# Decays in their own stage, the last product of block zero later, and scan products in two pieces

## The chip, the cores and the metric

The kernel runs on one core of one Trainium2 chip. The metric is the device time of one execution in microseconds; each kernel is run several times and the median counts. The engines are named as in the profile: PE is TensorE's matmul side and PEld its weight loads, DVE is VectorE, ACT is ScalarE, POOL is GpSimd, SP is SyncE, which here only issues DMAs. Each engine works through its own queue in order; semaphores tie the queues together.

## What is computed

A Mamba-2 scan (4 batches, 8 heads, 768 tokens, head size 32, state size 16) and then, on its output seen as 3072 tokens of 256 values, a two-layer network with an ELU between the layers:

```python
for c in range(nc):                      # chunks of tokens, per batch and head
    cum = np.cumsum(la, axis=-1)         # la = log(a)
    L = np.exp(cum[:, :, :, None] - cum[:, :, None, :]) * causal
    M = np.einsum('bhin,bhjn->bhij', Cc, Bc) * L
    y_intra = np.einsum('bhij,bhjd->bhid', M, xc)
    y_inter = np.einsum('bhin,bhnd->bhid', Cc, state) * np.exp(cum)[:, :, :, None]
    y[:, :, sl] = y_intra + y_inter
    state = decay_full * state + sum_j(Bc * xc * decay_from_j)
...
h = x @ w_in                             # 3072 x 256 by 256 x 2048
g = np.where(h > 0, h, np.exp(np.minimum(h, 0)) - 1)
out = g @ w_out                          # 3072 x 2048 by 2048 x 256
```

The weights come as 64-bit floats; the kernel reads them as two 32-bit words and makes 32-bit floats of them itself.

## The kernel before

**Blocks.** The 3072 tokens are 12 blocks of 256 (n = 0 to 11), each with all 8 heads of one batch. Blocks 0 to 3 go singly, then in pairs (4, 5), (6, 7), (8, 9), (10, 11). The order of all work is written out by hand: the kernel sets its own schedule, and each engine runs its instructions in the order in which the program issues them.

**The scan of a block.** `spread_cum` (L377) has SP load the tile L, the running sums of the logarithms spread over 128 partitions, from a scratch tensor `flat`. `decay_of(n, h)` (L518) turns one head of L into decays: two ACT activations at L521, and after every fourth head two causal masks on POOL at L526; `decay(n, q)` does two heads. L has two buffers. `scores` (L532) forms the products of C and B on PE (L541) and `weigh` (L546) multiplies them by L on DVE (L550) into M. `sums` and `states` carry the state along (PE L571, DVE L588, POOL L593). `across` (L604) multiplies the carried state on PE (L616) into four PSUM tiles ps_y, and `inside` (L624) adds the products of M and x to the same tiles (L635), first for t = 0 and then for t = 1 (four heads each), and copies each half out into yT with ACT (L652). `turn_part` transposes and masks B and C on DVE (L453, L461, L444), and `scaled` (L402) scales B on POOL (L408).

**The weights.** They come in 16 pieces. `w_take(i, low)` takes the two words apart: |high word| on ACT (L196), the low word on the engine that it is given (L205 on ACT or L209 on DVE), the sign on DVE (L223). `w_give` puts them together: DVE L231 and L238, then POOL L248. `words_of_w` (L731) and `low_of_w` (L741) split a finished piece of w_in into two words for the first layer of the pairs: ACT L736, DVE L737 and POOL L843.

**The first layer.** For single blocks `l1` (L659, PE L667) followed by `elu` (ACT L680, L687, DVE L689). For pairs `l1_words(n, m)` (L777): six matmuls at L787 into two PSUM tiles (ps_w and ps_h), ACT L791, then DVE L808 of the step before (`end_words`), DVE L794, and with `begin_end` ACT L800 and L801. It reads words of y that `words_of_y` (L750: ACT L755, DVE L759, L762) and `both_of_y` (DVE L772) make.

**The second layer.** `l2(n, j)` (PE L827) for blocks 0 and 1, with an ACT copy (L833) and a store at the end of a block. For pairs `second` (L866) is a generator of small steps of four matmuls each (L902), with sums of its operands on POOL (L843) and of its results on DVE (L880).

**The order around the change.** The loop over j = 0 to 7 (L1171) runs the second layer of block 0 (`l2(0, j)`) beside the first layer of blocks 2 and 3, takes the last pieces of w_out (at j = 0, 2, 3, 4 and 5), and calls `scan_ahead` (L1139), which prepares the scan of blocks 4 and 5. The loop over j = 8 to 15 (L1216, with i = j - 8) runs the first layer of the pair (2, 3). Then comes one stage for each pair, n = 4, 6, 8, 10 (L1298), of 16 steps k: `l1_words(n, k)`, `turn_step`, `stage_scan(n, k)` for the pair m = n + 2 (L1277), `begin_end`, and some steps of `second(n - 2)` by `l2s`. In step 9 the pair m is scored and weighed, in step 13 come `across` and `inside`. In step 10 `stage_scan` loads the tile L of the pair after m, and in steps 11 and 12 it computes that pair's first two `decay`s.

PSUM has seven buffers with the tag "a", shared by the tiles of the first layer, every second product sum of the second layer, and the scan's tiles; an eighth holds the other product sums.

Of the kernel before, what the change touches and what calls it, by code (L numbers as in the profile page):

```python
# [32 lines left out]
def kernel(  # L33
# [27 lines left out]
    nc = tc.nc  # L61
# [3 lines left out]
    NP = NB * NG  # L65
# [35 lines left out]
    st = {}  # L101
# [411 lines left out]
    def decay(n, q):  # L513

        decay_of(n, 2 * q)
        decay_of(n, 2 * q + 1)
# [104 lines left out]
                            tile_position=(32 * q, col), skip_group_check=True)  # L621
        return y

    def inside(y, *ns):  # L624


        for t in range(2):
            for at, n in enumerate(ns):
                s = st[n]
                for u in range(2):  # L630
                    for v in range(2):
                        toks = slice(Q * v, Q * v + Q)
                        for q in range(4):
                            h, col = 4 * t + q, (D * q + shift(n, v)) % P
                            nc.tensor.matmul(  # L635
                                out=y[t][v][col:col + D, at, u],
                                lhsT=s["x"][toks, u, D * h:D * (h + 1)],
                                rhs=s["M"][h // 2][toks, u, h % 2], start=False, stop=True,
                                tile_position=(Q * v, col), skip_group_check=True)
            n = ns[0]  # L640
            if n // 2 not in yT:
                yT[n // 2] = ffn.tile([P, KC, 2, 2, P], F32, tag="yT", name="yT")
            out = yT[n // 2][:, t, n % 2:n % 2 + len(ns)]
            for v in range(2):
                k = shift(n, v)
                for at in (0, k) if k else (0,):
                    count, src = P - k, (at + k) % P
                    to, src = out[at:at + count, :, :, Q * v:Q * v + Q], y[t][v][src:src + count]
                    if t and n == 1:
                        nc.vector.tensor_copy(to, src)  # L650
                    else:
                        nc.scalar.copy(out=to, in_=src)  # L652
        for n in ns:
            st.pop(n)


    g_of = {}
# [73 lines left out]
    def words_of_w(i):  # L731

        w = pieces[i][0]
        k_words[i] = conv.tile(
            [P, 2, KC, CW], F32R, tag="w64", name="w_words", bufs=W_AHEAD)
        nc.scalar.activation(k_words[i][:, 0], w, ACT.Copy, scale=NEAR)  # L736
        nc.vector.scalar_tensor_tensor(  # L737
            out=k_words[i][:, 1], in0=k_words[i][:, 0].bitcast(F32), scalar=1.0 / WORD - 1.0,
            in1=w, op0=ALU.mult, op1=ALU.add)
# [224 lines left out]
    def w_take(i, low):  # L964

        w_abs(i)
        w_low(i, low)
        w_sign(i)
# [38 lines left out]
    y = across(0)  # L1007
# [81 lines left out]
    todo = 5  # L1089
# [49 lines left out]
    def scan_ahead(i):  # L1139

        m = 4
        if i < 2:
            load_b(m + i)
            load_bc(m + i)
            spread_exp(m + i)
        if i == 2:
            spread_cum(5)
            load_x(m)
            load_x(m + 1)
        if 1 < i < 8:  # L1150
            decay(m + i // 6, (i - 2) % 4)
        for part in {3: (0,), 4: (1,), 6: (2, 0), 7: (1,)}.get(i, ()):
            turn_part(m + (i // 6 if part < 2 else 0), part)

# [15 lines left out]

    for j in range(2 * DIRECT):  # L1171
        n, i = 2 + j // DIRECT, j % DIRECT
        l2(0, j)
        piece = todo < len(pieces) and j != 1
        if j == 0:
            elu()
        if piece:
            w_take(todo, nc.scalar if j > 1 else nc.vector)
        l1(n, i)
        if j == 0:  # L1180
            scaled(3, nc.gpsimd)
            turn(3)
            elu()
            turn_exp(3)
        if piece:
            w_give(todo)
            todo += 1
        while lag:
            elu()
        if j == 0:  # L1190
            decay(3, 2)
            decay(3, 3)
        if j == 1:
            scores(3)
            sums(3)
            for q in range(4):
                weigh(3, q)
        if j == 2:
            states(3)
        if j == 3:  # L1200
            inside(across(3), 3)
        if j == 4:
            words_of_y(2)
        if j == 5:
            both_of_y(2)
        scan_ahead(j)
        if j == 3:
            s_out[:] = weight_sums()
        if j == 5:
            words_of_w(4)  # L1210
        if j == 6:
            low_of_w(4)
            differences(0, 4)
        if j == 7:
            words_of_w(5)
    for j in range(8, 16):  # L1216
        i = j - 8
        l1_words(2, j)
        if i == 7:
            words_of_y(4)  # L1220
        for p in ((), (6,), (), (7,), (0,), (1,), (2,), ())[i]:
            words_of_w(p)
        for p in ((5,), (), (6,), (7,), (0,), (), (), ())[i]:
            low_of_w(p)
        if i < 2:
            decay(5, i + 2)
        if i == 7:
            l2(1, 6)
            l2(1, 7)
        begin_end()  # L1230
        if i == 0:
            turn_part(5, 2)
            scaled(4, nc.gpsimd)
            scaled(5, nc.gpsimd)
        if i < 2:
            load_bc(i + 6)
            l2(1, i)
        if i == 2:
            turn_part(4, 3)
            turn_part(5, 3)  # L1240
            scores(4, 5)
            sums(4, 5)
            for q in range(4):
                weigh_two(4, q)
            l2(1, 2)
            states(4)
            states(5)
            for to in (6, 7):
                load_b(to)
                spread_cum(to)  # L1250
        if i == 3:
            l2(1, 3)
        if i == 4:
            l2(1, 4)
            y = across(4, 5)
            inside(y, 4, 5)
        if i == 5:
            l2(1, 5)
        if i in (0, 1, 3, 4):
            sum_t1(2, (0, 1, 3, 4).index(i), nc.vector)  # L1260
        if i in (4, 6):
            turn_part(6, i // 2 - 2)
        if i in (2, 5):
            differences(4 if i == 2 else 6, 2)
        if i < 6:
            sum_weights(nc.gpsimd, a_out, s_out, i)
# [10 lines left out]
    def stage_scan(n, k):  # L1277

        m = n + 2
        if k < 2:  # L1280
            spread_exp(m + k)
        if k == 2:
            load_x(m)
            load_x(m + 1)
        for h in range((5 + 3 * k) // 2, (8 + 3 * k) // 2) if 0 < k < 9 else ():
            decay_of(m + h // NH, h % NH)
        if k in (11, 12) and m + 2 < NP:
            decay(m + 2, k - 11)
        if k in (7, 8):
            scaled(m + k - 7, nc.gpsimd)  # L1290
        if k in (6, 7) and m + 2 < NP:
            load_bc(m + k - 4)
        if k == 10 and m + 2 < NP:
            for to in (m + 2, m + 3):
                load_b(to)
                spread_cum(to)

    for n in range(4, NP, 2):  # L1298
        m = n + 2 if n + 2 < NP else None
        steps = second(n - 2)  # L1300

        def l2s(count):
            for _ in range(count):
                next(steps)

        for k in range(16):
            l1_words(n, k)
            if m and k == 15:
                words_of_y(m)
            turn_step(n, k // 2 * 2 + 1, k % 2)  # L1310
            if n == 4 and k == 0:
                decay(6, 1)
            if n == 4 and 1 < k < 5:
                for _ in range(2):
                    next(left)()
            if m:
                stage_scan(n, k)
            begin_end()
            if k == 0 and n > 4:
                store(n - 4, 0)  # L1320
                store(n - 4, 1)
            if not m:
                l2s(4 if k % 2 else 3)
                continue
            l2s((3 + (n == 4), 3 - (n == 4), 3, 3, 3, 3, 3, 3, 4, 5, 2, 2, 3, 1, 3, 0)[k])
            if k == 9:
                scores(m, m + 1)
                sums(m, m + 1)
                for q in range(4):
                    weigh_two(m, q)  # L1330
                l2s(2)
                states(m)
            if k == 10:
                states(m + 1)
            if k == 13:
                y = across(m, m + 1)
                l2s(2)
                inside(y, m, m + 1)
        if m:
            l2s(4)  # L1340
            both_of_y(m)
        end_words()
        for _ in steps:
            pass
    n = NP - 2
# [34 lines left out]
```

## Time and profile before

| | us |
|---|---|
| median of 3 runs (352.72 to 353.66) | 353.25 |
| the profiled execution | 352.38 |
| its span | 350.4 |
| PE busy | 341.2 |
| DVE busy | 258.3 |
| ACT busy | 237.7 |
| POOL busy | 216.8 |

The span runs from the first to the last instruction in the trace; the profiled execution's own time has 2.0 us around it. PE's granted clock is full in the whole span. A row of the timeline has the start and the time in us, the engine, the line and operation, what it writes and reads, the number of like instructions in a row, and in brackets how long the engine was idle before it and what released it. PE's times are pipelined: one matmul lasts longer than the step to the next.

### The profile page before, as it was taken

What the parts mean: (1) busy time and instruction counts of PE and PEld (TensorE: products, weight loads), DVE (VectorE), ACT (ScalarE), POOL (GpSimd) and SP (SyncE); (2) the same over time, 40 slices, a digit from 0 to 9 for tenths busy, and PEclk for the clock granted to TensorE, in tenths of its full rate; (3) what the DMA queues carried; (4) which work ended last, traced back from release to release, by engine and by line L of the source; (5) the groups of instructions that cost most, each with busy time, mean ns of one, the idle gap of its engine ahead of it and who ended that gap; (6) DMA issues with size and microseconds to landing.
All of it is one profiled execution on the core that took longest, in us unless ns stands there. A gap on an engine that the chain in (4) does not pass through costs nothing.

```text
span 350.4 us, 9866 instructions
## 1 busy us (share of the span) xinstructions
PE 341.2 (97%) x3878; PEld 299.1 (85%) x3878; DVE 258.3 (74%) x511; ACT 237.7 (68%) x541; POOL 216.8 (62%) x338
## 2 busy tenths in 40 slices
PE   8899999999999999999999999999999999999996
PEld 5578888887778899888889988998988999999996
DVE  3998979879997898855878775888684757565232
ACT  4789989797668889567599467589547566665000
POOL 5554554539999699965196766095854074355860
PEclk9999999999999999999999999999999999999999
DMA  8978988461250510170431070230000100001001
GB/s 152 266 183 220 266 188 216 117 107 54 54 137 2 123 44 18 13 155 4 105 61 32 9 159 4 83 54 2 2 0 4 63 0 3 0 0 38 25 1 61
DMA packets 72726, 26.48 MB, mean 76 GB/s; under 512 B 57768, under 2 KB 67560, under 8 KB 72680
## 3 DMA queue, kind: packets, MB, share of 16 engines
q1 hardware_dynamic: 70360, 25.60, 31.3%
q8 instruction: 30, 0.49, 0.6%
q10 hardware_dynamic: 2320, 0.26, 0.5%
q14 instruction: 16, 0.13, 0.1%
HBM read 22.51 MB, written 3.34 MB: 74 GB/s over the span
## 4 chain that ended last, share of the span: by engine, by line
PE 62%; ACT 10%; DVE 7%; SPq 6%; DMA 5%; POOL 5%; issue 4%; POOLq 0%; ACTq 0%; DVEq 0%
PE ps_o L902 27%; PE ps_h L787 12%; PE ps_h L667 7%; PE ps_w L787 7%; PE ps_o L827 3%; DMA L<-flat 3%; SPq L116 2%; ACT L L521 2%; SPq L178 2%; PE ps_y L635 2%; ACT e L800 2%; DVE ps_h L794 2%; ACT e L801 1%; POOL g L843 1%; DMA bc<-in_C_dram 1%
## 5 line engine op out<-in xcount | busy, mean ns | idle before, releaser
L902 PEld LDWEIGHTS ps_o<-w_out,g 128*128 128x128 f32 x640 | 78.6, 192 | 3.4
L902 PE MATMUL ps_o<-w_out,g 128*128 128x128 f32 x640 | 80.1, 276 | 0.0
L808 DVE SCALAR_TENSOR_TENSOR g<-e,ps_h 128x512 f32<-128x512 f32 x72 | 49.3, 685 | 33.4 <-ACT e L801 32.9
L800 ACT ACTIVATE e<-ps_h 128x512 f32<-128x512 f32 x72 | 43.0, 597 | 44.6 <-DVE ps_h L794 44.6
L843 POOL TENSOR_TENSOR g<-g 128x256 f32<-128x256 f32 x36 | 26.3, 731 | 55.1 <-DVE g L808 55.1
L794 DVE SCALAR_TENSOR_TENSOR ps_h<-ps_h,e 128x512 f32<-128x512 f32 x72 | 50.1, 695 | 12.5 <-ACT e L791 9.5
L791 ACT ACTIVATE e<-ps_w 128x512 f32<-128x512 f32 x72 | 42.2, 586 | 20.0 <-PE ps_w L787 19.9
L787 PE MATMUL ps_w<-y_both,w_words 128*128 128x512 f32 x144 | 52.2, 440 | 0.5 <-DVE M L550 0.2
L801 ACT ACTIVATE e<-e 128x512 f32<-128x512 f32 x72 | 45.5, 631 | 2.3
L667 PE MATMUL ps_h<-yT,w_in 128*128 128x256 f32 (+1 forms) x208 | 45.3, 368 | 1.6 <-POOL w_in L248 1.6
L787 PE MATMUL ps_h<-y,w_words 128*128 128x512 f32 x144 | 45.6, 398 | 0.0
L787 PE MATMUL ps_h<-y,w 128*128 128x512 f32 x144 | 44.6, 391 | 0.0
L521 ACT ACTIVATE L<-L,ncum 128x64 f32<-128x64 f32 x160 | 42.8, 337 | 2.2 <-DMA L<-flat 1.5
L667 PEld LDWEIGHTS ps_h<-yT,w_in 128*128 128x128 f32 x208 | 36.5, 191 | 7.1 <-POOL w_in L248 2.3
L902 PE MATMUL ps_o<-w_sum,g 128*128 128x128 f32 x304 | 38.5, 276 | 0.1
L902 PEld LDWEIGHTS ps_o<-w_sum,g 128*128 128x128 f32 x304 | 37.1, 192 | 1.6 <-ACT e L791 0.5
L526 POOL TENSOR_SCALAR_AFFINE_SELECT L<-L 64x512 f32<-64x512 f32 x40 | 28.5, 712 | 14.3 <-ACT L L521 13.0
L787 PEld LDWEIGHTS ps_h<-y,w 128*128 128x128 f32 x144 | 27.1, 188 | 6.3
L787 PEld LDWEIGHTS ps_h<-y,w_words 128*128 128x128 f32 x144 | 26.8, 188 | 6.1 <-issue 0.4
L843 POOL TENSOR_TENSOR g<-t,g 128x256 f32<-128x256 f32 x40 | 28.1, 736 | 5.8 <-PE ps_o L902 5.7
L827 PE MATMUL ps_o<-w_out,g 128*128 128x256 f32 x128 | 30.5, 383 | 0.5 <-POOL w_out L248 0.5
L843 POOL TENSOR_TENSOR g<-g,t 128x256 f32<-128x256 f32 x40 | 29.6, 773 | 0.0
(134 smaller groups left out, 540.7 us busy)
## 6 DMA issues: line engine op xcount, KB each, us to landing
L<-flat SPq DMA_DIRECT2D x20, 256.0 KB
w<-in_moe_w_out_dram SPq DMA_DIRECT2D x8, 512.0 KB
w<-in_moe_w_in_dram SPq DMA_DIRECT2D x7, 512.0 KB
xr<-in_x_dram SPq DMA_DIRECT2D x24, 128.0 KB
out_dram<-c_sum SPq DMA_DIRECT2D x9, 256.0 KB
bc<-in_B_dram SPq DMA_DIRECT2D x24, 64.0 KB
bc<-in_C_dram SPq DMA_DIRECT2D x22, 64.0 KB
ec<-flat_exp SPq DMA_DIRECT2D x10, 128.0 KB
```

Of the source, the lines that this page charges most:

```text
L521: nc.scalar.activation(L[:, h, u], L[:, h, u], ACT.Exp, bias=ncum[:, u, row:row + 1])
L526: nc.gpsimd.affine_select(out=part, in_=part, pattern=[[0, 4], [0, 2], [1, Q]], compare_op=ALU.is_ge, fill=0.0, base=0, channel_multiplier=-1)
L667: nc.tensor.matmul(out=ps[:, j, toks], lhsT=w_in[i][:, k, j * P:(j + 1) * P], rhs=yT[n // 2][:, k, n % 2].rearrange("p u i -> p (u i)")[:, ...
L787: nc.tensor.matmul(out=ps, lhsT=lhs[:, k], rhs=rhs[:, k], start=k == 0 and lhs is not w0, stop=k == KC - 1 and lhs is not w1)
L791: nc.scalar.activation(e, both, ACT.Copy, scale=WORD)
L794: nc.vector.scalar_tensor_tensor(out=high, in0=high, scalar=WORD - 1.0, in1=e, op0=ALU.mult, op1=ALU.add)
L800: nc.scalar.activation(e, high, ACT.Relu, scale=-1.0)
L801: nc.scalar.activation(e, e, ACT.Exp, scale=-1.0)
L808: nc.vector.scalar_tensor_tensor(out=g_of[n, m].rearrange("p b i -> p (b i)"), in0=e, scalar=1.0, in1=h, op0=ALU.subtract, op1=ALU.max)
L827: nc.tensor.matmul(out=o_of[n][:, ts], lhsT=g_of[n, j][:, m % 2, ts * P:(ts + 1) * P], rhs=w_out[:, m], start=(m == 0 and ts == 0), stop=( ...
L843: nc.gpsimd.tensor_tensor(out=out, in0=in0, in1=in1, op=ALU.subtract)
L902: nc.tensor.matmul(out=ps[:, ts], lhsT=b[:, ts * P:(ts + 1) * P], rhs=a[:, i], start=(i == chunk[0] and ts == 0), stop=(i == chunk[-1]), s ...
```

## The change

- `inside` can be called for one t alone. In step 13 of the stages n = 4, 6 and 8 the two steps of the second layer that stood between `across` and `inside` are parted: one ahead of each half of `inside`.
- In the stages n = 6 and 8 all 16 heads of the pair m are decayed in steps 1 to 8, two in each. Before, four of them came in steps 11 and 12 of the stage before, and the other 12 in steps 1 to 8. Stage n = 4 keeps its 12 heads, and has no decays in steps 11 and 12.
- The eight decays of blocks 4 and 5 all come in the loop over j = 2 to 7 (1, 2, 1, 2, 1, 1 of them); before, six came there, one each, and two in the next two steps (i = 0, 1).
- In that loop the low words of the pieces at j = 2 to 5 are made by DVE, not by ACT; `words_of_w(4)` comes at j = 4 and `low_of_w(4)` at j = 5 (before: at the end of j = 5, and at j = 6); and `l2(0, 7)` comes behind `l1(3, 3)`.

The number of instructions on PE is the same. On DVE there are four more and on ACT four fewer.

```diff
-    def inside(y, *ns):
-        for t in range(2):
+    def inside(y, *ns, t=None):
+        for t in range(2) if t is None else (t,):
...
-        for n in ns:
-            st.pop(n)
+        if t:
+            for n in ns:
+                st.pop(n)
...
     def scan_ahead(i):
-        if 1 < i < 8:
-            decay(m + i // 6, (i - 2) % 4)
+        for q in {2: (0,), 3: (1, 2), 4: (3,), 5: (4, 5), 6: (6,), 7: (7,)}.get(i, ()):
+            decay(m + q // 4, q % 4)
...
     for j in range(2 * DIRECT):
         n, i = 2 + j // DIRECT, j % DIRECT
-        l2(0, j)
+        if j < 7:
+            l2(0, j)
         piece = todo < len(pieces) and j != 1
         if j == 0:
             elu()
         if piece:
-            w_take(todo, nc.scalar if j > 1 else nc.vector)
+            w_take(todo, nc.vector)
         l1(n, i)
+        if j == 7:
+            l2(0, j)
...
         if j == 4:
             words_of_y(2)
+        if j == 4:
+            words_of_w(4)
+        if j == 5:
+            low_of_w(4)
         if j == 5:
             both_of_y(2)
         scan_ahead(j)
...
-        if j == 5:
-            words_of_w(4)
         if j == 6:
-            low_of_w(4)
             differences(0, 4)
...
-        if i < 2:
-            decay(5, i + 2)
...
     def stage_scan(n, k):
-        for h in range((5 + 3 * k) // 2, (8 + 3 * k) // 2) if 0 < k < 9 else ():
+        heads = ((5 + 3 * k) // 2, (8 + 3 * k) // 2) if n == 4 else (2 * k - 2, 2 * k)
+        for h in range(*heads) if 0 < k < 9 else ():
             decay_of(m + h // NH, h % NH)
-        if k in (11, 12) and m + 2 < NP:
-            decay(m + 2, k - 11)
...
             if k == 13:
                 y = across(m, m + 1)
-                l2s(2)
-                inside(y, m, m + 1)
+                l2s(1)
+                inside(y, m, m + 1, t=0)
+                l2s(1)
+                inside(y, m, m + 1, t=1)
```

## The prediction

> **What bounds the kernel now.** I read the page's busy times first, then the timeline of PE alone from 45 us on, then the waits of the stretches in which PE pauses, then the timelines of ACT, DVE and POOL there.
>
> ```profile
> PE 341.2 (97%) x3878; PEld 299.1 (85%) x3878; DVE 258.3 (74%) x511; ACT 237.7 (68%) x541; POOL 216.8 (62%) x338
> ```
>
> PE is the bound: only its pauses can be won. Taking each MATMUL's start less the usual step between its kinds (111 ns between two L902 products, 146 ns from L635 to L787), the pauses after 45 us are 0.7 at 79.6, 0.5 at 92.5, 0.8 at 95.5, 0.7 at 104.4, 0.5 at 115, 1.7 from 156 to 160.6, 0.4 at 170, 0.95 from 210 to 214, 0.15 at 222 and 0.8 at 267: 7.2 us, the most that any reordering can bring. Three rows of PE's timeline, with the idle time and its releaser behind them, are the ones to know:
>
> ```profile
> 79.64 2.00 PE L827 MATMUL ps_o<-w_out,g 128*128 128x256 f32 x8 [0.53 <-POOL w_out L248]
> 157.26 0.68 PE L616 MATMUL ps_y<-bct,Sx 32*64 32x64 f32 x36 [0.51 <-DVE p_sum L880]
> 267.13 0.46 PE L635 MATMUL ps_y<-M,xr 64*32 64x64 f32 x33 [0.62 <-issue]
> ```
>
> **Part 1: no decays of the next pair in steps 11 and 12 of stage n = 4.** ACT and DVE there, from their timelines:
>
> ```profile
> 153.34 1.07 ACT L521 ACTIVATE L<-L,ncum 128x64 f32<-128x64 f32 x4 [1.52 <-DMA L<-flat]
> 155.46 0.58 ACT L791 ACTIVATE e<-ps_w 128x512 f32<-128x512 f32 x1
> ```
> ```profile
> 152.10 0.69 DVE L794 SCALAR_TENSOR_TENSOR ps_h<-ps_h,e 128x512 f32<-128x512 f32 x1
> 155.59 0.69 DVE L808 SCALAR_TENSOR_TENSOR g<-e,ps_h 128x512 f32<-128x512 f32 x1 [2.79 <-ACT e L801]
> 156.79 0.42 DVE L880 TENSOR_TENSOR p_sum<-ps_o,p_sum 128x256 f32<-128x256 f32 x1
> ```
>
> ACT reaches step 11's decays, waits 1.52 us for a transfer of L that was issued only at 148.1, and everything behind it in its queue (L800, L801, the next L791) is late; so DVE's L808, L794 and L880 are late; and L880 frees the PSUM buffer that PE's products at L616 want, hence the pause at 157.26. Without the decays: DVE's L794 ends at 152.79, L800 starts at 152.85 instead of 154.31, the next L791 at 154.0 instead of 155.46, L794 at 154.7, L880 at 155.3 to 155.7, before the 155.99 at which PE begins L616. PE then runs L616 without a pause, as it does in stage n = 8, which has no such decays: there the stretch from the step before L616 (262.86) to step 14 (267.52) takes 4.66 us, in n = 4 5.55 (155.46 to 161.01); n = 4 has 16 products of 13 ns fewer (0.2). Step 14 starts at about 160.05: 0.95 won. ACT's copies out of ps_y start at 159.25 instead of 160.70, so y_both is 1.45 earlier, PE only 0.95, and the 0.37 at 170 goes to about 0.05. Together 1.3 us, with 0.8 (L880 still a little late) and 1.6 as ends. What is late next is the fetch pause of part 4, counted in the 4.66.
>
> **Part 2: the same removal in stage n = 6.** Here it brings nothing: the decays lie in a wait that is there anyway.
>
> ```profile
> 206.67 1.06 ACT L521 ACTIVATE L<-L,ncum 128x64 f32<-128x64 f32 x4 [0.49 <-POOL Sx L593]
> 207.67 0.60 ACT L800 ACTIVATE e<-ps_h 128x512 f32<-128x512 f32 x1
> ```
> ```profile
> 206.94 0.69 DVE L794 SCALAR_TENSOR_TENSOR ps_h<-ps_h,e 128x512 f32<-128x512 f32 x1
> 210.17 0.42 DVE L880 TENSOR_TENSOR p_sum<-ps_o,p_sum 128x256 f32<-128x256 f32 x1
> ```
>
> L794 ends at 207.63, so L800 can't start before 207.67 with or without decays; DVE is late on its own, after eight L550 and eight L588. I take 0, with 0.4 as the end (that pause gone).
>
> **Part 3: 16 heads instead of 12 in steps 1 to 8 of n = 6 and n = 8.** Four L521 take 0.95 us and lie where ACT waits for L794. A step with four runs 2.60 us from L791 to L791 (176.32 to 178.92), one with two 2.63 (173.44 to 176.32, less 0.25 for the L914 copy in it); PE's step is 2.72. So 0; if that cover failed, 0.25 a step in four more steps, less the 0.1 of slack in each, would cost 0.6 a stage. POOL gets two L526 (1.4 us) more between 178 and 200, where it idles about 4 us (1.96 and 2.06 are its two longest); its next queue entry, four L843, ends at 182.6 instead of 181.1, and PE wants it at 187.98. 0.
>
> **Part 4: the scan products in two pieces.** PE's pauses within L635 (0.28, 0.47 and 0.83 in the three stages) have no releaser but "issue".
>
> ```profile
> q8 instruction: 30, 0.49, 0.6%
> ```
>
> These are 30 packets of 16 KB; one starts in the trace at 211.72 and PE resumes 2.37 us later, one at 264.47 and it resumes 2.66 later: PE has run through its instructions before the next block is there. The split puts four of eight L902 products later, but all eight are still between the start of that packet and the pause, so PE resumes at the same time. The one change of kind added (205 ns into L635, 146 out, less the steps saved: 0.23 us) goes into the pause; so does the 0.16 pause at 212.1. I take 0. Ends: 0.7 lost (3 x 0.23, not covered), 1.3 won (both later pauses gone). The Trainium skill, Runtime: NRT & Kernel Launch, Instruction fetch mechanics, says that blocks of 256 instructions are fetched while the one before runs and that this is mostly hidden. By that rule there is no pause to hide the 0.23 in, and the sum would be 0.7 lower; the rows above speak against it.
>
> **Part 5: loop of block zero, 57 to 97 us.** The change moves four low words (L205, 0.75 each) from ACT to DVE (L209: 0.42 median, 0.87 longest), puts L737 of w_words(4) ahead of the last w_out piece on DVE, puts eight L521 (2.0) instead of four into ACT at j = 3 and 5, and block zero's last product behind l1(3,3), 1.73 us later.
>
> ```profile
> 71.76 0.43 DVE L231 TENSOR_SCALAR mag<-mag 128x512 f32<-128x512 f32 x1 [1.61 <-ACT mag L196]
> 77.48 0.69 DVE L238 SCALAR_TENSOR_TENSOR mag<-mag,sgn 128x512 uint32<-128x512 uint32 x1
> 78.31 1.28 POOL L248 TENSOR_TENSOR w_out<-mag,w_out 128x512 uint32<-128x512 uint32 x1 [3.62 <-DVE mag L238]
> ```
>
> Of the four L209 two hide in DVE's 1.61 idle. The L196 of j = 4 comes after eight L521 at about 72.05 instead of 71.06; from the L231 behind it (72.65) DVE runs without idle: the old 6.4 us to the end of L238, less 0.3 idle, plus L737 0.93 and one L209 0.45: 80.1. POOL's L248 ends at 81.4. The product, now due at 80.7, waits 0.7 again: the move of 1.73 is eaten, and l1_words(2, 8) starts at about 83.1 (83.01 before). Behind it ACT's ob copy and L680 are 0.45 late; SP's store waits on that copy, and behind it stand the loads of bc(6), first read at 104.6, so they are covered. Taking the two decays out of the next two steps gives ACT 0.45 back (L800 at 90.66 waits for L521, L794 was done at 90.17), so the products after the weighing (95.50) move by about 0.2 later. Without any DVE contention 0.6 earlier, with L209 at 0.87 and L737 at 1.23 2.0 later. I take 0.2 lost, near the median rows. The Trainium skill, SBUF: State Buffer, two separate sides, says that DVE in a two-port mode and POOL lock each other out for a whole instruction, which speaks against moving L209 to DVE. It agrees with two L772 that took 2.51 us beside POOL's L526 and 1.28 alone.
>
> **Sum.** 1.3 + 0 + 0 + 0 - 0.2 = 1.1 us. The profiled execution took 352.38 (span 350.4), 0.87 under the median of 353.25: 351.3 against itself, 352.1 as a median.
>
> **Rivals.** *More*: the split does end the fetch pauses, or the last product is no longer waited for (0.47 + 0.83, or 0.7, or both): 350.1 to 351.4. For it: the split spreads the small products; against: the pause depends on the packet, and the same products lie before it. *DVE becomes the bound at j = 4 and 5*: each us that L238 of the last piece ends after 80.1 goes to PE whole; from 1.3 us late on it eats the gain of part 1; at the upper price (2.0 for 0.2) the time is 353.9, and 355 if two L772 at 1.25 each and L737, next in DVE's queue and read by l1_words(2, 8), are late by another 1.1. For it: DVE has no idle from 74 to 84; against: POOL, the other side of contended rows, is idle from 74.7 to 78.3. *Nothing*: the 1.7 at 156 is kept by DVE as in n = 6: 353.3.
>
> **Numbers.** Mine (351.5 to 352.8) 0.57, more 0.21, DVE 0.15, nothing 0.07. A measurement can tell 0.3%, 1.06 us. Faster: 0.31 of mine and all of "more": 0.52. Slower than 354.3: DVE's upper end, 0.09. The same: 0.39. Range 350.7 to 353.7, which leaves out the low end of "more" and the top of "DVE".
>
> **What would show it.** Right: no DMA wait at L521, L616 in n = 4 unbroken, step 14 less than 5 us after step 13's last product; pauses in L635 still there in all three stages; L827's wait for L248 still there, near 80.7. Wrong: L635 unbroken; PE pauses at L787 in steps 1 to 9 of n = 6; l1_words(2, 8) a microsecond from 83.

## The result, and the profile after

The changed kernel takes **351.92 us** (median of 18 runs, 351.15 to 353.13), the kernel before 353.04 on the same chips (18 runs, 351.95 to 353.86): a ratio of **0.9974, 95% interval 0.9962 to 0.9985**, or 1.1 us less. The profiled execution took 351.6 us, its span is 349.5. PE is still the bound (first row: busy time, share, instructions), and the DMA wait at L521 is gone: the second row, of the costliest groups, ends with the idle time ahead of the group, 0.2 us in all, where it had been 2.2 with 1.5 of it for the load of L.

```profile
PE 340.5 (97%) x3878; PEld 298.1 (85%) x3878; DVE 259.7 (74%) x515; ACT 234.7 (67%) x537; POOL 217.2 (62%) x338
...
L521 ACT ACTIVATE L<-L,ncum 128x64 f32<-128x64 f32 x160 | 42.2, 336 | 0.2
```

The changed kernel's L634 is L635 of before and its L651 is L652; L616, L667, L787 and L902 keep their numbers. PE's timeline of the changed kernel has the rows that answer to those of before:

```profile
81.87 1.99 PE L827 MATMUL ps_o<-w_out,g 128*128 128x256 f32 x8 [1.01 <-POOL w_out L248]
...
91.50 0.50 PE L787 MATMUL ps_h<-y,w 128*128 128x512 f32 x1 [0.20 <-POOL w L843]
...
156.56 0.83 PE L616 MATMUL ps_y<-bct,Sx 32*64 32x64 f32 x48
...
160.22 0.46 PE L634 MATMUL ps_y<-M,xr 64*32 64x64 f32 x31 [0.34 <-issue]
...
213.16 0.65 PE L634 MATMUL ps_y<-M,xr 64*32 64x64 f32 x40 [0.49 <-issue]
...
265.80 0.46 PE L634 MATMUL ps_y<-M,xr 64*32 64x64 f32 x33 [0.24 <-issue]
```

L616 of n = 4 runs unbroken, all three pauses in the scan products are still there, block zero's last product waits longer than before (1.01, was 0.53), and one wait is new, at 91.50.

The single traces differ by up to 0.9 us before the first edit acts (PE's ninth product L827 starts between 54.98 and 55.84 in all traces of this study), and the last stage, which has no edit, varies by 0.5. So I compare stretches. *Loop*: from that ninth product to the `ps_w` product at 118.1, less the fetch pause at 104, which is there in every kernel. *n = 4*, *n = 6*, *n = 8*: between two `ps_w` products, the same ones in every kernel (154.31 to 177.44, 205.75 to 230.80 and 258.98 to 283.83 in the trace of before).

| us | loop | n = 4 | n = 6 | n = 8 | ratio of times to before (95%) |
|---|---|---|---|---|---|
| before | 61.99 | 23.12 | 25.05 | 24.85 | 1 |
| changed kernel | 62.65 | 21.63 | 24.79 | 24.72 | 0.9974 (0.9962 to 0.9985) |
| stage_decays | 61.97 | 21.80 | 24.85 | 24.71 | 0.9959 (0.9948 to 0.9971) |
| split_only | 62.03 | 22.54 | 25.25 | 24.88 | 1.0003 (0.9988 to 1.0017) |
| loop_only | 62.60 | 22.39 | 25.29 | 24.63 | 1.0012 (0.9996 to 1.0028) |
| no_loop | 61.99 | 21.64 | 24.85 | 24.95 | 0.9958 (0.9946 to 0.9970) |
| late_product | 62.00 | 21.72 | 24.84 | 25.01 | 0.9961 (0.9945 to 0.9976) |
| late_plus_decays | 61.76 | 21.63 | 25.12 | 24.71 | 0.9948 (0.9930 to 0.9967) |
| late_plus_low | 62.24 | 21.62 | 25.06 | 24.71 | 0.9962 (0.9946 to 0.9979) |
| late_plus_words | 62.22 | 21.75 | 24.91 | 24.72 | 0.9974 (0.9962 to 0.9986) |
| wide_split | 61.98 | 21.81 | 24.86 | 25.07 | 0.9980 (0.9965 to 0.9995) |
| wide_best | 61.72 | 21.81 | 24.85 | 25.07 | 0.9956 (0.9938 to 0.9974) |
| pre_split | 61.97 | 22.03 | 25.06 | 25.43 | 0.9992 (0.9980 to 1.0003) |
| two_chains | 61.98 | 21.91 | 24.37 | 24.84 | 0.9943 (0.9921 to 0.9965) |

The loop column repeats within 0.06 among kernels with the same loop, so 0.2 can be read there. Between the two traces of before and after the span fell by 0.93: n = 4 gave 1.49, n = 6 0.26, n = 8 0.13, and the loop took 0.66 back; the rest (the start 0.25 earlier, the pause at 104 0.16 longer, the end 0.39 longer) lies where nothing was changed.

### The profile page after: what moved, and what is told of

It is laid out like the page before. It is cut to its first block, busy times and chain, and to the rows that moved or that the text cites. A ratio compares the mean times of both kernels' runs of the same rounds, so it can differ in the third digit from the quotient of the medians.

```text
span 349.5 us, 9873 instructions
## 1 busy us (share of the span) xinstructions
PE 340.5 (97%) x3878; PEld 298.1 (85%) x3878; DVE 259.7 (74%) x515; ACT 234.7 (67%) x537; POOL 217.2 (62%) x338
## 4 chain that ended last, share of the span: by engine, by line
PE 83%; DVE 4%; POOL 3%; ACT 3%; SPq 2%; issue 2%; DMA 2%; POOLq 0%; DVEq 0%; ACTq 0%
PE ps_o L902 36%; PE ps_h L787 18%; PE ps_w L787 9%; PE ps_h L667 9%; PE ps_o L827 4%; PE ps_y L634 2%; PE ps_g L541 2%; DMA w<-in_moe_w_in_dram 2%; PE ps_y L616 1%; PE ps_st L571 1%; POOL L L526 1%; POOL w L843 1%; SPq L178 1%; DVE y L762 1%; POOL w_sum L843 1%
## 5 line engine op out<-in xcount | busy, mean ns | idle before, releaser
L902 PEld LDWEIGHTS ps_o<-w_out,g 128*128 128x128 f32 x640 | 78.5, 191 | 3.4
L902 PE MATMUL ps_o<-w_out,g 128*128 128x128 f32 x640 | 80.1, 275 | 0.0
L843 POOL TENSOR_TENSOR g<-g 128x256 f32<-128x256 f32 x36 | 26.5, 737 | 58.3 <-DVE g L808 58.2
L794 DVE SCALAR_TENSOR_TENSOR ps_h<-ps_h,e 128x512 f32<-128x512 f32 x72 | 50.1, 695 | 12.4 <-ACT e L791 9.1
L787 PE MATMUL ps_w<-y_both,w_words 128*128 128x512 f32 x144 | 51.5, 437 | 0.1
L667 PE MATMUL ps_h<-yT,w_in 128*128 128x256 f32 (+1 forms) x208 | 45.1, 367 | 1.6 <-POOL w_in L248 1.6
L787 PE MATMUL ps_h<-y,w_words 128*128 128x512 f32 x144 | 45.7, 399 | 0.0
L787 PE MATMUL ps_h<-y,w 128*128 128x512 f32 x144 | 45.0, 392 | 0.2 <-POOL w L843 0.2
L667 PEld LDWEIGHTS ps_h<-yT,w_in 128*128 128x128 f32 x208 | 36.4, 190 | 7.2 <-POOL w_in L248 2.3
L521 ACT ACTIVATE L<-L,ncum 128x64 f32<-128x64 f32 x160 | 42.2, 336 | 0.2
L902 PE MATMUL ps_o<-w_sum,g 128*128 128x128 f32 x304 | 38.6, 276 | 0.0
L902 PEld LDWEIGHTS ps_o<-w_sum,g 128*128 128x128 f32 x304 | 37.0, 192 | 1.4
L526 POOL TENSOR_SCALAR_AFFINE_SELECT L<-L 64x512 f32<-64x512 f32 x40 | 29.3, 732 | 9.6 <-ACT L L521 8.2
L787 PEld LDWEIGHTS ps_h<-y,w 128*128 128x128 f32 x144 | 27.0, 188 | 7.2 <-POOL w L843 0.7
L787 PEld LDWEIGHTS ps_h<-y,w_words 128*128 128x128 f32 x144 | 26.7, 188 | 6.2 <-issue 0.5
L843 POOL TENSOR_TENSOR g<-t,g 128x256 f32<-128x256 f32 x40 | 28.2, 738 | 5.8 <-PE ps_o L902 5.7
L827 PE MATMUL ps_o<-w_out,g 128*128 128x256 f32 x128 | 30.5, 382 | 1.0 <-POOL w_out L248 1.0
L843 POOL TENSOR_TENSOR g<-g,t 128x256 f32<-128x256 f32 x40 | 28.8, 751 | 0.2
```

The lines of the kernel that those rows point to most:

```text
L521: nc.scalar.activation(L[:, h, u], L[:, h, u], ACT.Exp, bias=ncum[:, u, row:row + 1])
L526: nc.gpsimd.affine_select(out=part, in_=part, pattern=[[0, 4], [0, 2], [1, Q]], compare_op=ALU.is_ge, fill=0.0, base=0, channel_multiplier=-1)
L667: nc.tensor.matmul(out=ps[:, j, toks], lhsT=w_in[i][:, k, j * P:(j + 1) * P], rhs=yT[n // 2][:, k, n % 2].rearrange("p u i -> p (u i)")[:, ...
L787: nc.tensor.matmul(out=ps, lhsT=lhs[:, k], rhs=rhs[:, k], start=k == 0 and lhs is not w0, stop=k == KC - 1 and lhs is not w1)
L794: nc.vector.scalar_tensor_tensor(out=high, in0=high, scalar=WORD - 1.0, in1=e, op0=ALU.mult, op1=ALU.add)
L827: nc.tensor.matmul(out=o_of[n][:, ts], lhsT=g_of[n, j][:, m % 2, ts * P:(ts + 1) * P], rhs=w_out[:, m], start=(m == 0 and ts == 0), stop=( ...
```

## The experiments

Each ran 5 to 12 times, beside runs of the kernel before on the same chip. Most have one line more ahead of L667 than before; their L668, L738, L788, L828, L844, L881 and L903 are what the text calls L667, L737, L787, L827, L843, L880 and L902, and so on.

### The three parts alone

**stage_decays** is the kernel before with the removal in steps 11 and 12.

```diff
-        for h in range((5 + 3 * k) // 2, (8 + 3 * k) // 2) if 0 < k < 9 else ():
+        heads = ((5 + 3 * k) // 2, (8 + 3 * k) // 2) if n == 4 else (2 * k - 2, 2 * k)
+        for h in range(*heads) if 0 < k < 9 else ():
             decay_of(m + h // NH, h % NH)
-        if k in (11, 12) and m + 2 < NP:
-            decay(m + 2, k - 11)
```

> The kernel before with one edit: in stages n = 6 and 8 all 16 heads are decayed in steps 1 to 8, and steps 11 and 12 of n = 4 and 6 have no decays (parts 1 to 3). My theory: the DMA wait at L521 goes, L616 in n = 4 runs unbroken, the stretch from the step before L616 to step 14 of n = 4 takes 4.6 us instead of 5.55, another 0.4 is won at the y_both wait about 10 us later, and nothing in n = 6 and 8: 1.3 to 1.4 us faster than the kernel before. Rival (nothing): DVE is late on its own as in n = 6, no gain, the stretch stays over 5.4.

Measured: 0.9959, that is 1.4 us faster, more than the changed kernel as a whole (its interval and that of the changed kernel overlap by a little). L616 in n = 4 is unbroken, and the stage is 1.32 shorter. But PE now comes to the scan products earlier than their instructions, and the pause there is the longest of all n = 4 stages (1.0 by the prediction's way of counting, 0.2 to 0.7 in the others that have one): what was late next took part of the gain.

```profile
156.28 0.83 PE L616 MATMUL ps_y<-bct,Sx 32*64 32x64 f32 x48
...
160.11 0.46 PE L635 MATMUL ps_y<-M,xr 64*32 64x64 f32 x31 [0.78 <-issue]
```

**split_only** is the kernel before with the two pieces of `inside`.

```diff
-                l2s(2)
-                inside(y, m, m + 1)
+                l2s(1)
+                inside(y, m, m + 1, t=0)
+                l2s(1)
+                inside(y, m, m + 1, t=1)
```

> The kernel before with one edit: inside in two pieces with one step of the second layer ahead of each (part 4). My theory: the pauses within the scan products are set by the instruction packet, so PE resumes 2.4 to 2.7 us after a packet starts with or without the split; 0 us, pauses of 0.3 to 0.8 still in all three stages. Rival (more): the pauses go, 1.3 us faster. Rival (no pause to hide in): the added change of kind costs 0.23 in each of three stages, 0.7 slower.

Measured: 1.0003, no gain and no loss. The pauses are there in all three stages; against their instruction packets (157.69, 211.60 and 264.17 in this trace) PE goes on 2.43, 2.27 and 2.56 us later. The trace has one more thing to teach. Its n = 4 is 0.58 shorter than that of before, and the split isn't the reason: the wait of ACT for the load of L was shorter by chance.

```profile
152.75 1.06 ACT L521 ACTIVATE L<-L,ncum 128x64 f32<-128x64 f32 x4 [0.92 <-DMA L<-flat]
```

In loop_only, which has the same code in this stage, the group starts at 153.33 after 0.87 us, with POOL as its last releaser, and n = 4 is 0.73 shorter. So the one profile of before showed this wait at 1.52, the longest of the three; against the other two traces with these decays (22.54 and 22.39) the seven without them down to late_plus_words in the table are 0.6 to 0.9 shorter in n = 4, not 1.5.

**loop_only** is the kernel before with part 5, and **no_loop** the changed kernel without it.

```diff
+        for q in {2: (0,), 3: (1, 2), 4: (3,), 5: (4, 5), 6: (6,), 7: (7,)}.get(i, ()):
+            decay(m + q // 4, q % 4)
...
+        if j < 7:
+            l2(0, j)
...
+            w_take(todo, nc.vector)
         l1(n, i)
+        if j == 7:
+            l2(0, j)
...
+        if j == 4:
+            words_of_w(4)
+        if j == 5:
+            low_of_w(4)
```

> The kernel before with the edits of the loop over j = 0 to 7 alone (part 5: low words on DVE, words_of_w(4) early, decays of blocks 4 and 5 inside the loop, block zero's last product behind l1(3,3)). The trace of the changed kernel stood 0.5 to 0.6 us behind at 116 us, so my theory now: 0.5 slower than before, PE waits 0.7 to 1.2 for L248 at about 81 and a new 0.4 for w of L843 at about 91. The prediction on record had 0.2 slower. Rival: the loop part is a gain (the wait for L248 goes), 0.3 to 0.7 faster, and the 0.5 in the changed kernel's trace came from its start.

> The changed kernel with all edits of the loop over j = 0 to 7 taken back (parts 1 to 4 alone). My theory: 1.4 us faster than before, 0.5 faster than the changed kernel; to 116 us its trace goes as that of before. Rival (loop part is neutral or a gain): as fast as the changed kernel, 1.1 faster than before, or slower than that.

Measured: loop_only 1.0012, no_loop 0.9958. In the traces the loop takes 62.60 with part 5 and 61.99 without it. The timed ratio of no_loop and that of the changed kernel overlap by a little, and loop_only's interval holds 0.6 us more as well as no change; so the 0.6 rest on the traces, two with part 5 (62.60 and 62.65) and seven with the loop of before (61.97 to 62.03).

The trace of the changed kernel shows where part 5 loses: DVE, then POOL.

```profile
74.24 1.11 DVE L759 TENSOR_SCALAR y<-yT 128x512 fp32r<-128x512 f32 x1
75.38 1.75 DVE L762 SCALAR_TENSOR_TENSOR y<-y,yT 128x512 fp32r<-128x512 f32 x2
77.06 1.14 DVE L737 SCALAR_TENSOR_TENSOR w_words<-w_words,w_in 128x512 fp32r<-128x512 f32 x1
...
79.71 0.69 DVE L238 SCALAR_TENSOR_TENSOR mag<-mag,sgn 128x512 uint32<-128x512 uint32 x1
```
```profile
73.79 1.27 POOL L248 TENSOR_TENSOR w_out<-mag,w_out 128x512 uint32<-128x512 uint32 x1 [1.40 <-DVE mag L238]
75.67 2.00 POOL L526 TENSOR_SCALAR_AFFINE_SELECT L<-L 64x512 f32<-64x512 f32 x2 [0.60 <-ACT L L521]
...
80.55 1.27 POOL L248 TENSOR_TENSOR w_out<-mag,w_out 128x512 uint32<-128x512 uint32 x1 [2.89 <-DVE mag L238]
```

The decays that come earlier bring POOL's L526 to 75.67, beside DVE's L762 (1.75, was 1.29 before) and the first half of L737; L526 itself takes 2.00 there and 1.39 at 70.99. loop_only, late_plus_decays and wide_best, which have these decays too, also take 1.75 for L762. L759 (1.11, was 0.82) lies beside POOL's L248: in all 14 traces it ends 0.28 to 0.29 us after that L248 does, whether it has started 0.17 or 0.83 us before that end. L238 of the last piece ends 0.3 after the 80.1 that I had worked out, L248 at 81.82.

### Which edit of the loop loses

Each of these four adds edits of the loop to no_loop, so that the first has block zero's last product behind l1(3,3), and the other three have that and one more.

> The kernel of no_loop (parts 1 to 4 alone) with one of the loop's edits added: block zero's last product behind l1(3,3). My theory: L248 of the last piece still ends near 79.3, the product is now due at about 80.4, so the wait of 0.7 at L827 goes and l1_words(2, 8) starts about 0.7 earlier: 0.7 faster than no_loop, 2.1 faster than the kernel before. Rival: the PE wait only moves on (to y_both or the words that l1_words(2, 8) reads, DVE's L772 and POOL's L843 end near 81 to 83.6): no gain over no_loop.

Measured: 0.9961, as no_loop; the loop takes 62.00 against 61.99. L827 no longer waits, and the rival is right: the wait moves on by one row.

```profile
82.70 0.70 PE L788 MATMUL ps_w<-y_both,w_words 128*128 128x512 f32 x2
...
84.41 0.50 PE L788 MATMUL ps_h<-y,w 128*128 128x512 f32 x1 [0.31 <-POOL w L844]
```

PE's start is 0.23 late at 82.70 and 0.47 at 84.41, by the rule of the prediction (start to start, less the usual step), together the 0.7 that was to be won. `low_of_w(4)` makes that `w` on POOL from 82.11 on, behind L248 and L526.

> late_product with the decays of blocks 4 and 5 inside the loop as in the changed kernel (two at j = 3 and at j = 5, none in the two steps behind). Theory: L196 of j = 4 and so L231, L238 and L248 come 1.0 later, L248 ends at about 80.3, just as the product is due: wait 0 to 0.2 at L827; and the pauses at the sums and at the step behind weighing (0.45 and 0.6 at 92 to 95.5) shrink to 0.2 each: 0.3 to 0.6 faster than late_product. If this edit is what makes the loop part lose, the wait at L827 is 0.5 or more.

Measured: 0.9948, loop 61.76, 0.24 less than late_product. Of the wait at L827 0.1 is left, but l1_words(2, 8) waits longer for the words of w; in return the pauses at the sums and behind the weighing (0.56 and 0.60 in late_product) are gone. The gain is below the 0.3 to 0.6 expected.

```profile
83.90 0.70 PE L788 MATMUL ps_w<-y_both,w_words 128*128 128x512 f32 x2 [0.78 <-DVE w_words L738]
```

> late_product with the low words of the pieces at j = 2 to 5 made by DVE (L209) instead of ACT. Theory: of the four L209 two lie on DVE's way to the last L238, which ends 0.5 later; L248 ends at about 79.8, still before the product is due: as late_product within 0.2. If DVE and POOL hinder each other more than that, L248 ends after 80.4 and the wait at L827 is back.

Measured: 0.9962, loop 62.24, 0.24 more than late_product, just outside the 0.2 expected, though L248 ends at 80.24, before the product is due. The loss is in a place that I had not looked at, 13 us ahead of it. PE's timeline of late_plus_low, then of late_product:

```profile
67.57 0.80 PE L616 MATMUL ps_y<-bct,Sx 32*64 32x64 f32 x32
```
```profile
67.47 0.49 PE L616 MATMUL ps_y<-bct,Sx 32*64 32x64 f32 x32
```

As the changed kernel's timelines have it, the L209 at j = 2 puts L238, then POOL's L248 and the L593 behind it later, and L593 makes the Sx that L616 reads. PE comes to L635 0.33 later there by this. The changed kernel and loop_only have the same at 67.

> late_product with words_of_w(4) at j = 4 and low_of_w(4) at j = 5. Theory: L737 (1.14 in the traces so far) comes ahead of the last piece on DVE, L238 ends 1.1 later, L248 at 80.4 to 80.7: a wait of 0 to 0.3 at L827, 0 to 0.3 slower than late_product. If this edit makes the loop part lose, the wait is 0.5 or more.

Measured: 0.9974, loop 62.22, 0.22 more than late_product, within the 0 to 0.3 expected, but not at L827: L248 ends at 80.4, and L827 and l1_words(2, 8) don't wait at all. Taken row by row against late_product, PE is 0.7 ahead behind l1_words(2, 8). It gives back 0.26 at 90.25, at the product that reads POOL's `w` (the changed kernel has its 0.41 there), and 0.1 at the sums (92.48), where PE waits for POOL too, and is still 0.25 ahead at 109.6, without the fetch pause. The loss comes behind that, 0.48 more than in late_product ahead of the `ps_w` product that reads y_both: DVE's L762, one of the chain to y_both, took 1.61 there and 1.29 in late_product. PE, then DVE:

```profile
115.89 1.10 PE L788 MATMUL ps_w<-y_both,w_words 128*128 128x512 f32 x2
```
```profile
113.62 1.61 DVE L763 SCALAR_TENSOR_TENSOR y<-y,yT 128x512 fp32r<-128x512 f32 x2 [0.23 <-ACT y L758]
```

So no single edit loses the 0.65. Added to the late product, which itself costs nothing, the low words cost 0.2, the decays win 0.2, and the early words win 0.25 up to 109.6 and cost 0.2 by the end of the loop; yet together they lose 0.65, all of it before 96. I read this as the early words needing the time on DVE and POOL that the early decays and L209 have taken; that is an argument and not shown, as pairs of edits weren't tried.

### The pauses in the scan products

In the records of the traces without further long products there, PE stops at the same places of its program whatever the kernel: behind its 4033rd, 5313th and 6593rd instruction (products, weight loads and the semaphore instructions among them counted together), which are 1280 = 5 x 256 apart. The packet starts 185 to 208 instructions ahead (129 in one case), and PE goes on 2.3 to 2.7 us after its start (2.89 once). So more long products among these should end the pauses. The fetch pause at 104 is the same kind of stop, behind the 2753rd instruction, another 1280 ahead; there the packet starts 283 to 292 instructions ahead and PE goes on 2.8 to 3.4 us after it, so this time isn't the same everywhere. (Counts are of records; the stops themselves are those with "issue" as the releaser.)

**wide_split**, on no_loop:

```diff
-            l2s((..., 4, 5, 2, 2, 3, 1, 3, 0)[k])
+            l2s((..., 4, 5, 2, 2, 3, 1, 1, 0)[k])
...
                 inside(y, m, m + 1, t=0)
-                l2s(1)
+                l2s(3)
                 inside(y, m, m + 1, t=1)
```

**wide_best** has the same in late_plus_decays.

> The kernel of no_loop (parts 1 to 4 alone) with three steps of the second layer between the halves of inside instead of one, and one instead of three in step 14: 12 products L902 (1.33 us) between the halves, not 4 (0.44). Theory: in all traces so far PE stops at the same instruction of its program (two of the stops are 1280 instructions apart, five blocks of 256) and goes on 2.3 to 2.6 us after the packet starts; the packet starts about 186 instructions ahead of the stop. Of those 186 nearly all are small scan products; 0.89 us more of L902 among them covers the pauses of 0.57, 0.42 and 0.71: they go or leave less than 0.2 each, 1.2 to 1.7 won; ACT's copies for t = 1 come about 0.3 later and may give back up to 0.3 in each of two stages at the y_both wait. Net 0.6 to 1.6 faster than no_loop. Rival (the packet only starts later or the stop moves): the pauses stay above 0.4 and the time is that of no_loop or up to 0.6 slower.

> late_plus_decays with the same three steps between the halves and one in step 14: theory, both gains together, 0.6 to 1.6 faster than late_plus_decays, 349 us or less; rival, no faster than late_plus_decays (350.2).

Measured: 0.9980 and 0.9956, no gain; yet the pauses are gone in all six stages. PE and ACT of wide_split:

```profile
157.91 1.60 PE L903 MATMUL ps_o<-w_sum,g 128*128 128x128 f32 x12
159.45 0.86 PE L635 MATMUL ps_y<-M,xr 64*32 64x64 f32 x64
...
168.20 1.10 PE L788 MATMUL ps_w<-y_both,w_words 128*128 128x512 f32 x2
```
```profile
160.28 1.14 ACT L652 COPY yT<-ps_y 128x256 f32<-128x256 f32 x3 [0.20 <-PE ps_y L635]
```

L635 runs its 64 products unbroken. The packet starts where it did (186 to 208 instructions ahead in all six stages), but PE is at the place of the stop only 2.65 to 2.98 us after it, so the packet theory holds. But the `ps_w` products at 168.20 take 1.10 instead of 0.62 (no_loop, 168.49): they read y_both, whose second half DVE ends at 168.74, and the second product starts at 168.80. Ahead of it lie DVE's L762, ACT's L755 and ACT's copies out of ps_y, all 0.2 later than in no_loop. In no_loop DVE ends at 168.55, and PE comes to the second product at 168.71: the pause for the packet and the chain to y_both end together, and the two steps that I took from step 14 were the cover of the chain.

**pre_split** takes the two steps from ahead of the scan instead (steps 7 and 8, one each).

> The kernel of no_loop (parts 1 to 4 alone) with three steps of the second layer between the halves of inside, as in wide_split, but taken from steps 7 and 8 (one each less), not from step 14. In wide_split the three pauses in the scan products went, and yet n = 4 took 0.2 longer than in no_loop: ACT's six copies out of ps_y end at 161.4, after them the chain to y_both (DVE, 168.7) was the last thing that l1_words(6, 0) waits for, and 0.9 of PE's work that covered it had been moved ahead. Theory: with the work taken from ahead of step 9, PE and that chain both come earlier (PE by the pause, the chain by 0.4 or more), so each of the three stages n = 4, 6 and 8 is 0.4 to 0.6 shorter: 1.2 to 1.7 faster than no_loop, span about 347.2. Rival: the chain to y_both is bound by ACT and DVE alone and comes no earlier, PE waits for it in place of the packet: within 0.3 of no_loop.

Measured: 0.9992, slower than no_loop. The pauses in L635 are 0.24 at most, but PE now waits at the sums in step 9, 0.85 to 0.92 in each stage, for M, which DVE's eight L550 make:

```profile
145.37 0.84 PE L571 MATMUL ps_st<-xr,b_tok 64*32 64x64 f32 x56 [0.64 <-DVE M L550]
```

Those two steps had been the cover of the weighing. The theory is right on the packet and wrong on where the time goes; the rival named a wait, but the wrong one.

**two_chains** shortens both at once: two steps between the halves and two in step 14, and the copies for t = 0 on DVE.

```diff
-                    if t and n == 1:
+                    if (t and n == 1) or (not t and n > 4):
                         nc.vector.tensor_copy(to, src)
```

> The kernel of no_loop (parts 1 to 4 alone) with two steps of the second layer between the halves of inside and two in step 14 (no_loop: one and three), and with the three copies out of ps_y for t = 0 on DVE instead of ACT in the stages n = 4, 6 and 8. Theory: in no_loop two things end together, PE's pause for the packet and the chain to y_both (ACT's six copies 158.93 to 161.25, y_both at 168.55, PE wants it at 168.49); shortening one alone gave nothing (wide_split). Here the packet's pause loses 0.44 of its 0.4 to 0.7, and ACT's copies for t = 1 start when PE ends the second half, at about 159.8, and end at 160.9, 0.35 earlier: 0.2 to 0.4 won in each of three stages, 0.6 to 1.2 faster than no_loop. Rival (a third limit, such as DVE's L808 and L794 behind the three copies): the time of no_loop within 0.3, or slower.

Measured: 0.9943, the lowest ratio of the study, though its interval (0.9921 to 0.9965) takes in no_loop. By the traces it is 0.27 slower in n = 4, 0.48 faster in n = 6 and 0.11 in n = 8 than no_loop, 0.3 in all instead of 0.6 to 1.2. In n = 6 the second half runs unbroken; in n = 4 the packet of this trace took 2.99 us until PE went on, and the pause stayed:

```profile
160.12 0.56 PE L635 MATMUL ps_y<-M,xr 64*32 64x64 f32 x35 [0.36 <-issue]
...
212.51 0.86 PE L635 MATMUL ps_y<-M,xr 64*32 64x64 f32 x64
```

So the two-chain reading is supported in n = 6, by one trace (24.37; the nine kernels of the table without the decays in steps 11 and 12, from the changed one down to wide_best, take 24.79 or more), and not settled in n = 4.

## Why the prediction was right, and where it was not

The median (351.9) is 0.2 from the 352.1 predicted, but two terms were off in opposite directions, and a third came out on a wait that another trace would have priced lower. That the sum came so close is luck; that parts 1, 3 and 4 went as worked out is not.

**Part 1, right.** The DMA wait, the late L880 and the pause at L616 went together. Step 14's start is 0.98 earlier by difference (0.95 predicted; the trace stands 0.57 behind ahead of it and 0.41 ahead behind it), the whole stage 1.49 shorter (1.3, end 1.6). DVE's L880 now ends before PE's L616 (156.56) starts, as worked out:

```profile
155.28 0.69 DVE L794 SCALAR_TENSOR_TENSOR ps_h<-ps_h,e 128x512 f32<-128x512 f32 x1
155.88 0.41 DVE L880 TENSOR_TENSOR p_sum<-ps_o,p_sum 128x256 f32<-128x256 f32 x1
```

That the size came out is partly luck: the wait that I priced was 1.52 in the one trace I had, and 0.92 and 0.87 in two others.

**Part 2, mis-sized: 0 predicted, about 0.3 measured.** n = 6 takes 25.05 to 25.29 in the three traces with the decays, 25.20 in the mean, and 24.79 to 25.12 in the nine without them that differ there in the split or in `l2s` counts behind step 9 at most, 24.90 in the mean. Less the fetch pause in L635, which goes its own way (0.4 to 1.0), the two groups lie apart: 24.58 to 24.74 with the decays, 24.05 to 24.42 in the seven without them that have the pause. The step that failed is "DVE is late on its own": in the changed kernel L794 ends 0.29 earlier against PE's step, since a gap of 0.46 ahead of the last L588 is gone too, and the pause of 0.32 at L616 with it. Before:

```profile
206.15 0.28 DVE L588 SCALAR_TENSOR_TENSOR S_new<-S_new,ec,ps_st 128x64 f32<-128x64 f32 x1 [0.46 <-DVE S_new L588]
```

All three traces with the decays have such a gap ahead of an L588 (0.46 or 0.47), none of the nine without them has more than 0.19. I had kept this as the end of 0.4. The gap ends before ACT starts the decays of step 11 (206.67), so it isn't they themselves that hold this L588; what does wasn't tried and stays open.

**Part 3, right.** From 174 to 205 us the traces of before and after keep the same 0.92 to 0.93 between them, so the eight L521 more in each stage cost PE nothing; n = 8 is 0.13 shorter.

**Part 4, right**, and tested by itself (1.0003). The Trainium skill, Runtime: NRT & Kernel Launch, Instruction fetch mechanics, has 16 KiB blocks of 256 instructions and calls the crossing mostly hidden. The block size agrees with the 1280 instructions between two stops; "hidden" doesn't, where these are small products: PE stood 0.2 to 1.0 us there in all three stages of every trace with at most one step between the halves. As wide_split shows, ending the pauses by moving this work won nothing: the chain to y_both had ended at the same time.

**Part 5, the sign right, the size wrong: 0.2 predicted, 0.65 measured.** Three things failed in it. L759 and L762 were taken at their rows of before, with POOL idle from 74.7 to 78.3; but the earlier decays put L526 there, beside L762, L759 lies longer beside L248, and L737 was taken at 0.93 and took 1.14; so L248 ended at 81.8 instead of 81.4 and PE waited 1.17, not 0.7. The L209 at j = 2 was priced in DVE's queue, not in POOL's behind it (0.3 at 67). And POOL's queue behind the late L248, which starts 2.24 later than before (80.55, was 78.31) with as many masks and words behind it, wasn't followed to low_of_w(5): its `w` ends at 91.45 and made a new wait of 0.41 at 91.5. The pauses at 93 and 95.5 shrank by 0.64, more than I had counted. The Trainium skill, SBUF — State Buffer, SBUF: two separate sides, would have POOL and a DVE operation (in a two-port mode, or with two inputs in SBUF) wait for each other by whole instructions; the traces agree. L759 always ends 0.28 to 0.29 us after L248; and in the four traces with the early decays L526 and L762 take turns: the first L526 ends 0.52 after the first L762, the second L762 0.54 after that, the second L526 0.52 to 0.53 after that; where L737 is next (the changed kernel and loop_only), it ends 0.54 after that again.

**Rivals.** *DVE becomes the bound at j = 4 and 5* was the right place, at a third of its upper price. *More* fell: the pauses stayed, and the last product still waited. *Nothing* fell with stage_decays.

## What to carry to other kernels

A load that lands just in time has no fixed price: take such a wait from more than one trace before its removal is priced. Where PE is 97% busy, a wait removed shows the next one, a few rows on: late_product won 0.7 at one row and lost it at the next two; wide_split and pre_split won most of three pauses and gave them back where the moved work had been a cover. So ask of each piece of work that is moved what it hid where it was, and shorten all chains that end at one point, or none.

## What the runs showed of the hardware

- PE stops for instructions at fixed places of its program, 1280 instructions apart here, and goes on 2.3 to 2.7 us after the packet starts (2.89 and 2.99 in one case each, 2.8 to 3.4 at 104); 0.9 us more of long products among the 200 ahead of the stop ended the pause.
- The same stop costs 0.2 to 1.0 us from one trace to the next with nearly the same code around it, and a load that one trace waits 1.52 us for, another waits 0.92 for; so 0.5 us in such a stage between two single profiles is no difference.
- DVE's L762 beside POOL's L526 took 1.75 us instead of 1.29 (four traces), and L526 up to 2.00 instead of 1.39: their instructions end in turn, 0.52 to 0.54 us apart. DVE's L759 beside POOL's L248 took 0.46 to 1.12 us and ended 0.28 to 0.29 us after it in all 14 traces.
